# Loading K in pairs of tiles of 64 KB per partition and transposing it in place in a five-region buffer (gated attention and MLP mix, decode, one core)

## The chip, the cores and the metric

The kernel runs on one core of one Trainium2 chip. The metric is the time of one execution in microseconds of device time, the median over several runs. The span of a profile is a little shorter than the time, since it starts with the first instruction. PE is the matrix engine, PEld its weight load, DVE the vector engine, ACT the scalar engine, POOL the gpsimd engine, SP the engine that issues nearly all loads here.

## The reference, cut to what matters

```python
x = A_x                                             # (1, 1, 1024)
g = sigmoid((x * gate_w).sum(-1, keepdims=True))
# a: one query, 32 heads on 4 key/value heads, 65536 keys of 128, bf16
q = (x @ wq) ...                                    # wq (1024, 4096)
scores = einsum('bhqd,bhkd->bhqk', q, k) * 128 ** -0.5
o = softmax(scores) @ v
a = o.reshape(1, 1, 4096) @ wo                      # wo (4096, 1024)
# b: gated MLP on the same x: w_in (1024, 3584), w_out (1792, 1024)
return g * a + (1 - g) * b
```

K and V are 67 MB each. With the weights the kernel has to read 162 MB and writes 2 KB.

## The kernel before

One tile is 128 keys in each of 128 partitions, 32 KB per partition, 4 MB. A head has NT = 4 tiles. All large loads go through one buffer, `kv`, of NKV = 4 regions of one tile each.

```python
NKV = 4
...
ktp = ctx.enter_context(tc.tile_pool(name="ktp", bufs=3))
...
kv = big.tile([P, NKV * CT * P], BF16, name="kv")

def load_kv(src, g, j, at, n=1):          # n tiles, into region `at` and on
    k0, m = j * CT * P, n * CT
    v = load(src[0, g, k0:k0 + m * P, :].rearrange("(p c) d -> p (c d)", c=m),
             (m * DH,), at)
    return [v[:, i * CT * DH:(i + 1) * CT * DH] for i in range(n)]

def k_tile(g, j, kn):                     # scores of one tile
    kb = kn.bitcast(I32)
    n = CC * DH // 2
    s_ps = pss.tile(...)
    for v in range(VC):                   # VC = 4
        kt = ktp.tile([P, CC * DH], BF16, name="kt")
        nc.vector.transpose(out=kt[:].bitcast(I32), in_=kb[:, v * n:(v + 1) * n])
        ...
        kx = kt[:].rearrange("p (c h k e) -> p h e c k", h=2, k=B, e=2)
        ...                               # 8 matmuls on kx, into s_ps
    ...                                   # ACT copies s_ps to bf16 scores

def stats(g): ...                         # maximum over the head, exponentials, transposed
def v_tile(g, j, vt): ...                 # 32 matmuls with V as the moving operand
def head_out(g): ...                      # picks and sums the blocks of one head's output

for g in range(G):                        # 4 heads
    for j in range(NT):
        k_tile(g, j, load_kv(A_k_cache, g, j, (j - 1) % NKV if g == 0 else j % 2)[0])
        ...
        if j == NT - 1:
            stats(g)
        if g > 0 and j % 2 == 1:          # V of the head before, two tiles at once
            for i, vt in enumerate(load_kv(A_v_cache, g - 1, j - 1, 2, 2)):
                v_tile(g - 1, j - 1 + i, vt)
    if g > 0:
        head_out(g - 1)
for j, n, at in ((0, 2, 0), (2, 1, 2), (3, 1, 3)):   # V of the last head
    ...
```

From the second head on, K takes turns in regions 0 and 1, tile by tile, and V comes in pairs into regions 2 and 3. So V's packets are 64 KB (one run per partition) and K's are 32 KB. A wait on a region stands in SP's instruction stream, ahead of the load that overwrites it; a framework places these waits.

## Time and profile before

| | before |
|---|---|
| time, median of 3 runs | 383.88 us (383.83 to 383.91) |
| span | 382.1 us |
| bytes read, mean rate | 162 MB, 424 GB/s |
| PE, DVE busy | 62%, 57% |
| load queue, share of the 16 DMA engines' span | 98.7% |

From the page of before: busy time of each engine; two rows of the 40 slices of the span (DMA's busy share in tenths, and GB/s); the packet count; and the load queue's line (packets, MB, share of 16 engines).

```profile
PE 236.9 (62%) x1372; PEld 60.0 (16%) x796; DVE 218.7 (57%) x211; ACT 39.6 (10%) x55; POOL 4.4 (1%) x10
...
DMA  9999999999999999999999999899999999999995
GB/s 379 442 422 418 427 433 439 439 436 428 427 432 429 425 437 453 432 418 418 461 439 394 439 478 439 379 422 463 425 413 432 460 426 425 432 412 427 439 412 221
DMA packets 5239, 162.17 MB, mean 424 GB/s; under 512 B 616, under 2 KB 620, under 8 KB 1004
...
q1 hardware_dynamic: 5188, 162.01, 98.7%
```

DMA is at 9 or 8 tenths in every slice but the last; no compute engine is near that over the span. (Both rows count a packet whole in the slice in which it starts, so a slice can show more than the transfers' steady rate.) The kernel ends when its bytes have come, plus a short tail.

The groups of before that the change touches (line, engine, operation, tiles; busy us and mean ns of one; idle time just before them and what ended it):

```profile
L388 PE MATMUL s_ps<-kt,wt 128*128 128x512 bf16 x512 | 138.4, 428 | 63.5 <-DVE kt L382 63.3
L382 DVE STREAM_TRANSPOSE kt<-kv 128x2048 int32<-128x2048 int32 x64 | 142.7, 2280 | 39.5 <-DMA kv<-in_A_k_cache_dram 39.5
```

The waits of SP in before (who is waited for: total us, times, longest):

```profile
SPq L166 <- DVE kt L382: 170.5, 15, 18.1
SPq L166 <- DMA kv<-in_A_v_cache_dram: 41.0, 6, 10.2
SPq L166 <- PE o_ps L434: 39.7, 6, 9.3
```

These look large and cost nothing: SP waits while the transfers already issued keep all engines busy. The test for a wait of the issuer is whether the next transfer still starts where the last one ends, and here it does.

### The profile page before, as it was taken

How to read it: one execution, taken by the hardware profiler on the slowest of the kernel's cores; microseconds unless marked ns; L12 is line 12 of the kernel's file. 1: busy time of each engine (PE TensorE's matmuls, PEld its weight loads, DVE VectorE, ACT ScalarE, POOL GpSimd, SP SyncE). 2: the span in 40 equal slices, each digit the busy share in tenths (PEclk: the TensorE clock that was granted, in tenths of full speed). 3: DMA queues.
4: the chain of work that ended last, by engine and by line, in shares of the span. 5: the costliest groups of instructions: out<-in, count | busy, mean ns of one | idle time of the engine just before them, and what ended most of it. 6: DMA issues, size and time to landing. Idle time of an engine off the chain costs nothing.

```text
span 382.1 us, 2629 instructions
## 1 busy us (share of the span) xinstructions
PE 236.9 (62%) x1372; PEld 60.0 (16%) x796; DVE 218.7 (57%) x211; ACT 39.6 (10%) x55; POOL 4.4 (1%) x10
## 2 busy tenths in 40 slices
PE   0433457777257966774879485548776964539355
PEld 0110011111111211121112011211111111112123
DVE  4241477997498379555971586659804976400040
ACT  1010001110601101140011011400110105000000
POOL 4000000000000000000000000000000000000000
PEclk9999999998859899867689789897888996959768
DMA  9999999999999999999999999899999999999995
GB/s 379 442 422 418 427 433 439 439 436 428 427 432 429 425 437 453 432 418 418 461 439 394 439 478 439 379 422 463 425 413 432 460 426 425 432 412 427 439 412 221
DMA packets 5239, 162.17 MB, mean 424 GB/s; under 512 B 616, under 2 KB 620, under 8 KB 1004
## 3 DMA queue, kind: packets, MB, share of 16 engines
q1 hardware_dynamic: 5188, 162.01, 98.7%
q8 instruction: 8, 0.13, 0.1%
q14 instruction: 3, 0.02, 0.0%
q10 hardware_dynamic: 40, 0.01, 0.0%
HBM read 162.01 MB, written 0.00 MB: 424 GB/s over the span
## 4 chain that ended last, share of the span: by engine, by line
DMA 57%; PE 22%; DVE 15%; issue 3%; ACT 2%; SPq 0%; DVEq 0%; ACTq 0%
DMA kv<-in_A_v_cache_dram 31%; DMA kv<-in_A_k_cache_dram 14%; DVE kt L382 12%; PE o_ps L434 11%; PE s_ps L388 10%; DMA kv<-in_A_wo_dram 7%; DMA kv<-in_B_w_in_dram 5%; DVE pt L424 1%; ACT sc L399 1%; PE z_ps L275 1%; DVE o_sb L449 0%; SPq L166 0%; ACT L421 0%; ACT sc L421 0%; DVE om L445 0%
## 5 line engine op out<-in xcount | busy, mean ns | idle before, releaser
L388 PE MATMUL s_ps<-kt,wt 128*128 128x512 bf16 x512 | 138.4, 428 | 63.5 <-DVE kt L382 63.3
L382 DVE STREAM_TRANSPOSE kt<-kv 128x2048 int32<-128x2048 int32 x64 | 142.7, 2280 | 39.5 <-DMA kv<-in_A_k_cache_dram 39.5
L434 PE MATMUL o_ps<-kv,pt 128*64 128x512 bf16 x512 | 69.3, 437 | 22.4 <-DMA kv<-in_A_v_cache_dram 22.4
L388 PEld LDWEIGHTS <-wt 128*128 128x128 bf16 x256 | 27.1, 106 | 175.9 <-issue 138.1
L399 ACT CAST sc<-s_ps 128x1024 bf16<-128x1024 f32 x16 | 16.2, 1013 | 245.9 <-PE s_ps L388 245.9
L445 DVE TENSOR_TENSOR om<-o_ps,own 128x1024 f32<-128x1024 f32 x4 | 4.9, 1225 | 46.0 <-PE o_ps L434 46.0
L434 PEld LDWEIGHTS <-pt 128*64 128x64 bf16 x256 | 19.5, 125 | 69.9 <-issue 65.0
L424 DVE STREAM_TRANSPOSE pt<-sc 128x1024 bf16<-128x1024 bf16 x16 | 18.6, 1217 | 6.8 <-ACT sc L421 6.8
L384 DVE TENSOR_REDUCE mx<-sc 128x1 f32<-128x1024 bf16 x12 | 14.5, 1209 | 9.5 <-ACT sc L399 9.4
L421 ACT ACTIVATE sc<-sc,nb 128x1024 bf16<-128x1024 bf16 x16 | 18.2, 1136 | 9.6 <-DVE nb L417 9.6
L403 DVE TENSOR_REDUCE mx<-sc 128x1 f32<-128x1024 bf16 x4 | 4.9, 1220 | 13.6 <-ACT sc L399 13.6
L275 PE MATMUL q_ps<-kv,xT 128*32 128x512 bf16 x64 | 7.2, 630 | 7.3 <-DMA kv<-in_A_wq_dram 7.3
L455 PE MATMUL om_ps<-o_sb,hsel 128*32 128x128 f32 x8 | 2.1, 353 | 12.3 <-DVE o_sb L449 12.3
L275 PE MATMUL z_ps<-kv,xT 128*32 128x448 bf16 x64 | 6.4, 576 | 3.8 <-DMA kv<-in_B_w_in_dram 3.8
L476 PE MATMUL out_ps<-kv,oa 128*32 128x256 bf16 x128 | 6.5, 364 | 3.3 <-DMA kv<-in_A_wo_dram 1.9
L341 DVE TENSOR_TENSOR rowt<-q_ps,own_b 128x512 f32<-128x512 f32 x2 | 1.3, 686 | 12.4 <-PE q_ps L275 12.4
L449 DVE TENSOR_REDUCE o_sb<-om 128x128 f32<-128x1024 f32 x4 | 7.5, 1871 | 0.1
L407 PE MATMUL mt_ps<-ident_f,m 128*1 128x128 f32 x4 | 1.1, 270 | 8.5 <-DVE m L405 8.5
L515 ACT CAST out_sb<-out_ps 128x256 bf16<-128x256 f32 x1 | 0.4, 372 | 56.0 <-PE out_ps L476 56.0
L289 DVE TENSOR_TENSOR rowt<-z_ps,own_b 128x448 f32<-128x448 f32 x2 | 1.2, 618 | 8.6 <-PE z_ps L275 8.6
L275 PEld LDWEIGHTS <-xT 128*32 128x32 bf16 x64 | 3.0, 139 | 19.3 <-issue 19.2
L231 PE MATMUL xb_ps<-xg,spread 8*128 8x256 bf16 x1 | 0.4, 365 | 8.9 <-DMA xg<-in_gate_w_dram 8.9
(88 smaller groups left out, 58.6 us busy)
## 6 DMA issues: line engine op xcount, KB each, us to landing
kv<-in_A_k_cache_dram SPq DMA_DIRECT2D x16, 4096.0 KB, 24.9
kv<-in_A_wq_dram SPq DMA_DIRECT2D x2, 4096.0 KB, 32.7
kv<-in_A_v_cache_dram SPq DMA_DIRECT2D x2, 4096.0 KB
kv<-in_B_w_in_dram SPq DMA_DIRECT2D x2, 3584.0 KB, 18.7
kv<-in_A_wo_dram SPq DMA_DIRECT2D x1, 4096.0 KB
kv<-in_B_w_out_dram SPq DMA_DIRECT2D x1, 3584.0 KB
kv<-in_A_wo_dram SPq DMA_DIRECT2D x1, 2048.0 KB
kv<-in_A_wo_dram SPq DMA_DIRECT2D x1, 1024.0 KB
```

What stands on the lines that cost most here:

```text
L275: ins = nc.tensor.matmul(ps[t * B:(t + 1) * B, k * HN:k * HN + n], lhsT=xT[:, i * KH + c:i * KH + c + 1].to_broadcast([P, B]), rhs=w[:, c, ...
L382: nc.vector.transpose(out=kt[:].bitcast(I32), in_=kb[:, v * n:(v + 1) * n])
L384: nc.vector.reduce_max(**late.pop())
L388: ins = nc.tensor.matmul(s_ps[:, k * HN:(k + 1) * HN], lhsT=wt[g % 2][:, v, b].rearrange("p a v h -> p (a v h)"), rhs=kx[:, b // 2, b % 2, ...
L399: nc.scalar.copy(out=sct[g, j][:], in_=s_ps[:])
L403: nc.vector.reduce_max(**late.pop())
L421: nc.scalar.activation(out=sct[g, j][:], in_=sct[g, j][:], func=ACT.Exp, scale=SCALE, bias=nb[:, 0:1], accum_out=lss[g][:, j:j + 1])
L424: nc.vector.transpose(out=ptt[g, j][:].rearrange("p c x -> p (c x)"), in_=sct[g, j][:])
L434: ins = nc.tensor.matmul(o_ps[g][hs, e, :], lhsT=ptt[g, j][:, 2 * u:2 * u + 2, :].rearrange("p c x -> p (c x)"), rhs=vx[:, 2 * u + e], sta ...
L445: nc.vector.tensor_tensor(out=om8[:], in0=o_ps[g][:].rearrange("p e (v d) -> p (e v) d", d=DH), in1=own_8[:].unsqueeze(2).to_broadcast([P, ...
L449: nc.vector.tensor_reduce(out=o_sb[:], in_=om8[:].rearrange("p x d -> p d x"), axis=AX.X, op=ALU.add)
L476: nc.tensor.matmul(out_ps[t * B:(t + 1) * B, :], lhsT=vec[:, c0 + c:c0 + c + 1].to_broadcast([P, B]), rhs=w[:, c, t * NO:(t + 1) * NO], st ...
```

## The change

The intent: K too in packets of 64 KB. That takes a fifth region, and the room comes from the transposed copies (`ktp`, 24 KB per partition) and from one scratch tile: K is now transposed in place. A K pair of one half head lies in regions 1 and 2, the next in 0 and 1, so region 1 is shared and its tile is taken first each time; V lies in 3 and 4.

```diff
-NKV = 4
+NKV = 5
...
-    ktp = ctx.enter_context(tc.tile_pool(name="ktp", bufs=3))
...
-            kt = ktp.tile([P, CC * DH], BF16, name="kt")
-            nc.vector.transpose(out=kt[:].bitcast(I32), in_=kb[:, v * n:(v + 1) * n])
+            nc.vector.transpose(out=kb[:, v * n:(v + 1) * n], in_=kb[:, v * n:(v + 1) * n])
...
-            kx = kt[:].rearrange("p (c h k e) -> p h e c k", h=2, k=B, e=2)
+            kx = kn[:, v * CC * DH:(v + 1) * CC * DH].rearrange(
+                "p (c h k e) -> p h e c k", h=2, k=B, e=2)
...   (w_in, w_q and the first head's K go to other regions; om8 shares rowt)
+    for g in range(1, G):
+        for h in range(2):
+            kn = load_kv(A_k_cache, g, 2 * h, 1 - h, 2)
+            for i in ((0, 1), (1, 0))[h]:
+                k_tile(g, 2 * h + i, kn[i])
+            if h == 0 and g + 1 < G:
+                build_w(g + 1)
+            vn = load_kv(A_v_cache, g - 1, 2 * h, 3, 2)
+            v_tile(g - 1, 2 * h, vn[0])
+            if h == 1:
+                stats(g)
+            v_tile(g - 1, 2 * h + 1, vn[1])
+        head_out(g - 1)
+    for j, n, at in ((0, 2, 1), (2, 1, 3), (3, 1, 4)):
...
```

The first head's K stays in single tiles.

More of the change, by code (lines that the diff above doesn't have):

```diff
@@ L186 @@
     win_view = B_w_in.rearrange("(p c) n -> p c n", c=KC)
-    win_t = [load(win_view[:, i * KH:(i + 1) * KH, :], (KH, F), 2 + i) for i in range(2)]
+    win_t = [load(win_view[:, i * KH:(i + 1) * KH, :], (KH, F), 3 + i) for i in range(2)]
     wq_view = A_wq.rearrange("(p c) n -> p c n", c=KC)
-    wq_t = [load(wq_view[:, i * KH:(i + 1) * KH, :], (KH, HD), i) for i in range(2)]
+    wq_t = [load(wq_view[:, i * KH:(i + 1) * KH, :], (KH, HD), 1 - i) for i in range(2)]
     row = const.tile([P, P], FP32, name="row")
@@ L286 @@
     rowt = big.tile([P, 2 * HN], FP32, name="rowt")
+    om8 = rowt[:].rearrange("p (x d) -> p x d", d=DH)
     zm = rowt[:, :2 * ZN].rearrange("p (h j c) -> p h j c", h=2, c=FC)
@@ L395, in k_tile @@
                         same_weights(ins)
-        if j == 0:
+        if g not in mxs:
             mxs[g] = wk.tile([P, NT], FP32, name="mx")
@@ L443, in head_out @@
         gs = slice(g * B, (g + 1) * B)
-        om8 = big.tile([P, 2 * VC, DH], FP32, name="om8")
         nc.vector.tensor_tensor(
-            out=om8[:], in0=o_ps[g][:].rearrange("p e (v d) -> p (e v) d", d=DH),
+            out=om8, in0=o_ps[g][:].rearrange("p e (v d) -> p (e v) d", d=DH),
             in1=own_8[:].unsqueeze(2).to_broadcast([P, 2 * VC, DH]), op=ALU.mult)
         o_sb = wk.tile([P, DH], FP32, name="o_sb")
-        nc.vector.tensor_reduce(out=o_sb[:], in_=om8[:].rearrange("p x d -> p d x"), axis=AX.X,
+        nc.vector.tensor_reduce(out=o_sb[:], in_=om8.rearrange("p x d -> p d x"), axis=AX.X,
                                 op=ALU.add)
@@ L484 @@
     build_w(0)
-    for g in range(G):
-        for j in range(NT):
-            k_tile(g, j, load_kv(A_k_cache, g, j, (j - 1) % NKV if g == 0 else j % 2)[0])
-            if j == 1 and g + 1 < G:
+    for j in range(NT):
+        k_tile(0, j, load_kv(A_k_cache, 0, j, (2, 1, 0, 3)[j])[0])
+        if j == 1:
+            build_w(1)
+    project(load(B_w_out.rearrange("(p c) n -> p c n", c=FC), (FC, D), 4), FC, uT, 0, first=True)
+    stats(0)
+    for g in range(1, G):
[4 more added lines that the diff above has]
+            if h == 0 and g + 1 < G:
                 build_w(g + 1)
-            if g == 0 and j == NT - 1:
-                project(load(B_w_out.rearrange("(p c) n -> p c n", c=FC), (FC, D), 3),
-                        FC, uT, 0, first=True)
-            if j == NT - 1:
+            vn = load_kv(A_v_cache, g - 1, 2 * h, 3, 2)
+            v_tile(g - 1, 2 * h, vn[0])
+            if h == 1:
                 stats(g)
-            if g > 0 and j % 2 == 1:
-                for i, vt in enumerate(load_kv(A_v_cache, g - 1, j - 1, 2, 2)):
-                    v_tile(g - 1, j - 1 + i, vt)
-        if g > 0:
-            head_out(g - 1)
-    for j, n, at in ((0, 2, 0), (2, 1, 2), (3, 1, 3)):
+            v_tile(g - 1, 2 * h + 1, vn[1])
+        head_out(g - 1)
+    for j, n, at in ((0, 2, 1), (2, 1, 3), (3, 1, 4)):
         for i, vt in enumerate(load_kv(A_v_cache, G - 1, j, at, n)):
```

## The prediction

> **What bounds the kernel now.** The DMA engines, from first to last. The slices of the span show DMA at 9 in 39 of 40; the queue table gives the load queue 98.7% of the 16 engines' span, 162 MB at 424 GB/s. PE is 62% busy, DVE 57%. Packet records, laid out in order, show the next transfer starting where the last one ends, from 1.2 us to about 373 us. The long waits of the queue's own issuer (up to 18 us, on the K transposes) all end while earlier transfers still run, so they cost nothing. The Trainium skill, "DMA: Bandwidth & Descriptors", section "Bandwidth", derives a ceiling of 435 GB/s from the SBUF ports; this trace agrees: a 64 KB packet takes 2423 ns on average, which is 433 GB/s over 16 engines.
>
> **What the change does.**
> 1. K of heads 1 to 3 (50 MB) comes in 64 KB rather than 32 KB per partition. Packets: 32 KB take 1219 ns (430 GB/s), 64 KB 2423 ns. Two small ones cost 14.5 ns more than one large; 768 pairs over 16 engines are 48 each: 0.7 us. As a cross-check, two K transfers plus one V pair take 38.9 us from V end to V end, and a V pair alone 19.36 us, so a K pair costs 19.54 us; 0.18 us per pair, six pairs: 1.1 us. All of it is on the critical path. Six completions fewer: under 0.1 us.
> 2. A K region is now free only when the tile's matmuls end, not when its transposes end: about 2 us later (8 matmuls after the last transpose took 1.9 us). And a load of a pair needs its first region, so K issues come later relative to need.
> 3. The transposes no longer wait for a free kt buffer; their count, shape and expected cost (2269 ns) stay. K matmuls read the same pattern from another buffer. DVE and PE work is unchanged.
> 4. The first K load goes to an unused region and issues near 2 us instead of 22.8 us. Worth nothing: w_in and w_q keep the engines busy until 38 us.
>
> **Is the queue still fed?** Estimate from those durations. A K pair lands, four transposes (9.1 us) and the last matmuls (2 us) free the shared region, up to 1 us late behind the previous head's statistics: 12 us. The V pair ahead of the next K load occupies the engines for 19.4 us, and an issue needs about 1 us, landing another 1 us: some 5 us of slack. V loads: as now, issued when the pair's matmuls end, about 6 to 7 us ahead of need. So no starvation, though the K margin shrinks. The tail (V, w_o, projection, output) has the same bytes and order.
>
> **Prediction.** 383.0 us against 383.88; 8 in 10 between 382.2 and 384.0. Faster by over 2%: 1%; within 2%: 96%; slower by over 2%: 3%.
>
> **What would show it.** K of heads 1 to 3 as six issues of 8192 KB; 64 KB packets near 2420 ns; still 9 in every slice but the last; a K-plus-V cycle near 38.75 us instead of 38.9; the transposes still near 2270 ns; the queue's waits for K now ending on PE s_ps; the last w_o load landing about 1 us earlier.
>
> **What would make it wrong.** In-place transposes slower than 2.27 us: at 1.5 times the margin is just gone, at twice each of six pairs starves the queue by some 4 us. A slice of low granted clock that stretches a K or V tile past the 5 us of slack: a gap of 1 to 3 us, cancelling the gain. A skew between the 16 engines at the end (1.2 us now) that grows and eats it.

## More of the kernel before

A finer measure comes from the packet records themselves. Each transfer ends on each of its 16 engines with a 4-byte packet that reports completion. The first of the 16 reports comes from the engine that is furthest ahead, in general one that nothing else disturbed, so the distance between first reports of successive transfers is taken here as the undisturbed time of a transfer.

## The result, and the profile after

| | before | after |
|---|---|---|
| time, 6 runs each | 383.92 us (383.83 to 384.00) | 383.44 us (383.30 to 383.55) |
| ratio, 95% interval | | 0.9987 (0.9974 to 1.0) |
| span | 382.1 us | 381.7 us |

A ratio is the mean time of one kernel's fast runs over that of the other's fast runs of the same rounds, so it is not quite the ratio of the medians. Two later sets of five runs gave 383.57 against 383.97 us and 383.52 against 384.02 us, ratios 0.9989 and 0.9987. So the change gains 0.4 to 0.5 us, a little over 0.1%. Each interval taken alone just touches 1. But the 16 runs of after lie between 383.30 and 383.84 us, and the 24 runs of before beside them between 383.82 and 384.22 us, so the two hardly touch.

The page of after, in the same rows:

```profile
PE 229.4 (60%) x1372; PEld 56.6 (15%) x796; DVE 218.4 (57%) x211; ACT 39.6 (10%) x55; POOL 4.4 (1%) x10
...
DMA  9999999999999999999999999999999999999995
GB/s 376 438 419 422 433 435 440 433 471 415 407 426 440 440 441 426 440 433 440 440 428 440 440 440 433 434 427 426 412 433 441 433 440 413 428 419 433 433 414 220
DMA packets 4376, 162.17 MB, mean 425 GB/s; under 512 B 521, under 2 KB 525, under 8 KB 909
...
q1 hardware_dynamic: 4324, 162.01, 98.7%
```

The load queue has 864 packets fewer: 768 of data and 96 completion reports (six transfers, 16 engines). DMA is as busy as before. The transposes cost the same in place, in the groups of after:

```profile
L388 PE MATMUL s_ps<-kv,wt 128*128 128x512 bf16 x512 | 138.1, 427 | 85.4 <-DVE kv L381 85.4
L381 DVE STREAM_TRANSPOSE kv<-kv 128x2048 int32<-128x2048 int32 x64 | 142.7, 2280 | 58.8 <-DMA kv<-in_A_k_cache_dram 58.8
```

SP's waits in after; K's regions now come free in two steps, the transposes and then the matmuls (PE s_ps):

```profile
SPq L165 <- DVE kv L381: 140.3, 8, 21.1
SPq L165 <- DMA kv<-in_A_v_cache_dram: 48.3, 7, 8.1
SPq L165 <- PE o_ps L434: 38.3, 4, 11.2
...
SPq L165 <- PE s_ps L388: 14.6, 7, 2.6
```

When SP issued the loads of the second and third heads, from the timeline of SP in after (start us, length us, what):

```profile
118.12 0.33 SPq L165 DMA_DIRECT2D kv<-in_A_k_cache_dram  x1
136.71 0.33 SPq L165 DMA_DIRECT2D kv<-in_A_v_cache_dram  x1
158.08 0.33 SPq L165 DMA_DIRECT2D kv<-in_A_k_cache_dram  x1
178.11 0.33 SPq L165 DMA_DIRECT2D kv<-in_A_v_cache_dram  x1
196.49 0.33 SPq L165 DMA_DIRECT2D kv<-in_A_k_cache_dram  x1
```

Compared with the packet records, where the transfers ahead of these end (mean over the engines) at 124.73, 144.18, 163.54, 182.90 and 202.36 us, the loads come 6.6, 7.5, 5.5, 4.8 and 5.9 us early. Over the whole run K's least lead is 5.2 us and V's 4.8 us; counted from the first engine's end, which runs dry first, they are 4.5 and 4.2 us. From the start of an issue to its first packet 0.95 us pass (seen below, where engines were idle), so some 3 to 4 us are spare. The issue itself takes 0.33 us of it; the remaining 0.62 us agree with the about 0.6 us to the first byte that the Trainium skill gives, "DMA: Bandwidth & Descriptors", section "Specifications", if these are counted from the end of the issue, which that section doesn't say.

The undisturbed time of the transfers by first completion reports, in us (the 19.445 is the mean of six in k_two_loads below, whose K packets are those of before and where nothing disturbed that engine; before itself has the same 9.72 to 9.73 in eleven of twelve, and 9.88 in one, during which a fetch of instructions ran):

| | before | after |
|---|---|---|
| a K pair of heads 1 to 3 | 19.445 (two of 9.72 to 9.73) | 19.36 |
| a V pair | 19.36 | 19.36 |
| last report of the last w_o load, slowest engine | 378.94 | 378.48 |

A K pair gains 0.085 us, six of them 0.51 us; the last w_o load lands 0.46 us earlier, and the time fell by 0.48 us. That 0.46 lies so near to 0.51 is partly luck: the slow K load of before (0.16 us) and a first load that ended 0.15 us later in after happen to cancel. A cleaner sum is the time from the first report of the first load to that of the last V pair: 326.92 and 326.91 us in the changed kernel (after, after_third; 327.01 in after_again, with one K pair of 19.46), and 327.44 and 327.43 us in k_two_loads and in_place_alone, which have the packets of before.

### The profile page after: what moved, and what is told of

The parts are those of the page before. It is cut to its first block, busy times and chain, and to the rows that moved or that the text cites. A ratio compares the mean times of both kernels' runs of the same rounds, so it can differ in the third digit from the quotient of the medians.

```text
span 381.7 us, 2586 instructions
## 1 busy us (share of the span) xinstructions
PE 229.4 (60%) x1372; PEld 56.6 (15%) x796; DVE 218.4 (57%) x211; ACT 39.6 (10%) x55; POOL 4.4 (1%) x10
## 3 DMA queue, kind: packets, MB, share of 16 engines
q1 hardware_dynamic: 4324, 162.01, 98.7%
## 4 chain that ended last, share of the span: by engine, by line
DMA 60%; PE 20%; DVE 15%; issue 1%; ACT 1%; SPq 1%; DVEq 0%; ACTq 0%
DMA kv<-in_A_k_cache_dram 38%; PE s_ps L388 15%; DVE kv L381 9%; DMA kv<-in_A_wo_dram 8%; DMA kv<-in_A_wq_dram 7%; DMA kv<-in_A_v_cache_dram 7%; PE o_ps L434 3%; DVE pt L424 2%; DVE mx L383 1%; DVE o_sb L448 1%; PE q_ps L274 1%; ACT sc L421 1%; DVE rowt L444 1%; ACT sc L399 1%; SPq L165 1%
## 5 line engine op out<-in xcount | busy, mean ns | idle before, releaser
L388 PE MATMUL s_ps<-kv,wt 128*128 128x512 bf16 x512 | 138.1, 427 | 85.4 <-DVE kv L381 85.4
L381 DVE STREAM_TRANSPOSE kv<-kv 128x2048 int32<-128x2048 int32 x64 | 142.7, 2280 | 58.8 <-DMA kv<-in_A_k_cache_dram 58.8
L434 PE MATMUL o_ps<-kv,pt 128*64 128x512 bf16 x512 | 62.6, 404 | 7.5 <-DMA kv<-in_A_v_cache_dram 7.5
L434 PEld LDWEIGHTS <-pt 128*64 128x64 bf16 x256 | 16.2, 116 | 51.3 <-issue 48.4
L444 DVE TENSOR_TENSOR rowt<-o_ps,own 128x1024 f32<-128x1024 f32 x4 | 4.8, 1195 | 25.7 <-PE o_ps L434 25.7
L383 DVE TENSOR_REDUCE mx<-sc 128x1 f32<-128x1024 bf16 x12 | 14.5, 1206 | 7.0 <-ACT sc L399 7.0
L448 DVE TENSOR_REDUCE o_sb<-rowt 128x128 f32<-128x1024 f32 x4 | 7.5, 1872 | 0.1
L475 PEld LDWEIGHTS <-oa 128*32 128x32 bf16 x128 | 4.5, 129 | 5.5 <-issue 2.7
```

The source lines that it names most:

```text
L381: nc.vector.transpose(out=kb[:, v * n:(v + 1) * n], in_=kb[:, v * n:(v + 1) * n])
L383: nc.vector.reduce_max(**late.pop())
L388: ins = nc.tensor.matmul(s_ps[:, k * HN:(k + 1) * HN], lhsT=wt[g % 2][:, v, b].rearrange("p a v h -> p (a v h)"), rhs=kx[:, b // 2, b % 2, ...
L434: ins = nc.tensor.matmul(o_ps[g][hs, e, :], lhsT=ptt[g, j][:, 2 * u:2 * u + 2, :].rearrange("p c x -> p (c x)"), rhs=vx[:, 2 * u + e], sta ...
L444: nc.vector.tensor_tensor(out=om8, in0=o_ps[g][:].rearrange("p e (v d) -> p (e v) d", d=DH), in1=own_8[:].unsqueeze(2).to_broadcast([P, 2 ...
L448: nc.vector.tensor_reduce(out=o_sb[:], in_=om8.rearrange("p x d -> p d x"), axis=AX.X, op=ALU.add)
```

## The experiments

Theory 1: every packet costs the engine a fixed time beside its bytes, and the packets saved are the whole gain. Rival: the gain comes from the rest of the change, the five regions, the earlier first load, the transposes that need no free buffer. A second question was the price of the change: how much slack the later release of K's regions leaves. All outputs are right.

### after_again: the changed kernel once more

No edit.

> The changed kernel once more, to narrow its interval. Both theories: 383.4 us, 0.4 to 0.6 us under the kernel before. If the difference shrinks below 0.2 us, there is nothing to explain.

Measured: 383.57 us (383.49 to 383.76) against 383.97 us, ratio 0.9989 (0.9976 to 1.0001). The difference is there again.

### k_two_loads: only the packet size goes back

```diff
-            kn = load_kv(A_k_cache, g, 2 * h, 1 - h, 2)
+            kn = load_k_halves(g, 2 * h, 1 - h)   # two loads of 32 KB per partition,
+                                                  # same bytes into the same places
```

> The changed kernel with each K pair loaded by two transfers of 32 KB per partition into the same places, so buffer, order and in-place transposes stay. Theory 1 (each packet costs some 11 ns beside its bytes, and that is all the gain): 48 packets per engine come back, 0.5 to 0.6 us, so 383.9 to 384.1 us, as slow as the kernel before. Rival (the gain comes from the buffer of five regions, the earlier first K load and the transposes that need no free buffer): stays at 383.4 us.

Measured: 383.94 us (383.88 to 384.25), ratio 0.9999 (0.9987 to 1.0012). With the five regions, the pairs' order and the in-place transposes all kept, the gain is gone. Its page counts the packets of before again:

```profile
DMA packets 5239, 162.17 MB, mean 424 GB/s; under 512 B 616, under 2 KB 620, under 8 KB 1004
```

A pair took 19.445 us on the undisturbed engine. The rival is out, as far as these parts together are concerned. (Two transfers instead of one come with the smaller packets here; k_runs_4k, below, keeps the number of transfers.)

### in_place_alone: only the in-place transposes

```diff
 # on the kernel before, four regions, single K tiles
-            kt = ktp.tile([P, CC * DH], BF16, name="kt")
-            nc.vector.transpose(out=kt[:].bitcast(I32), in_=kb[:, v * n:(v + 1) * n])
+            nc.vector.transpose(out=kb[:, v * n:(v + 1) * n], in_=kb[:, v * n:(v + 1) * n])
```

> The kernel before with in-place transposes and nothing else: four regions, K in single tiles. Theory 1: nothing on the critical path moves, 383.8 to 384.0 us, equal to before; the transposes still take about 2270 ns. Rival (in place itself gains): below 383.6 us. If regions freed later at the end of the matmuls starve the queue: above 384.3 us.

Measured: 384.01 us (383.88 to 384.18), ratio 1.0 (0.9988 to 1.0013); the transposes took 2279 ns on average. In place is neutral. Its worth is the room that it frees; whether pairs could be had without it was not tried.

### k_runs_4k: many more packets in the same six transfers

```diff
-            kn = load_kv(A_k_cache, g, 2 * h, 1 - h, 2)
+            kn = load_k_runs(g, 2 * h, 1 - h, 16)  # src "(a p c) d -> p a (c d)", a=16
```

> The changed kernel with each K row of 64 KB cut into 16 runs of 4 KB, in the same single transfer (keys are permuted among partitions, which the sums do not show at these inputs). Theory 1: 120 more packets per engine in each of six transfers, 720 at 11 ns: 7.9 us more, 391.4 us, between 391 and 392; packets of 4 KB at 160 to 165 ns. Rival (packet size does not matter while the engines are fed): 383.4 to 384 us.

Measured: 390.18 us (390.09 to 390.28), ratio 1.0161 (1.0146 to 1.0177); 6.6 us more than after_again of the same call.

```profile
DMA packets 15895, 162.17 MB, mean 418 GB/s; under 512 B 520, under 2 KB 524, under 8 KB 13196
...
q1 hardware_dynamic: 15844, 162.01, 99.5%
```

The direction is theory 1's; the size is under its 7.9 us. A K transfer took 20.44 us on the undisturbed engine against 19.36: 1.08 us for 120 packets, 9.0 ns each, and six times 1.08 is the 6.5 us. The 11 ns had been read from the lengths of packet records, which overlap a little; by those lengths (164 ns for 4 KB, 128 of them) the transfer would have taken 20.99 us, which it didn't. Completion times are the better measure. The order in which addresses are read changed with the packets here, from one run of 64 KB to runs of 4 KB that lie far apart; what that does alone was not tried, but the 9.0 ns are close to what k_two_loads shows without it, 0.085 us for 8 packets and a completion report.

### v_two_loads: the opposite change on V

```diff
 # on the kernel before: each V pair as two loads of 32 KB per partition
+        if n == 2:
+            pair = src[0, g, k0:k0 + m * P, :].rearrange("(p c) d -> p c d", c=m)
+            return [load(pair[:, i * CT:(i + 1) * CT, :], (CT, DH), at + i)... for i in range(2)]
```

> The kernel before with its seven V pairs loaded as two transfers of 32 KB per partition each, the opposite of the change on the other cache. Revised cost of 9 to 10 ns for a packet more: 7 times 0.085 us, 0.6 us slower than the kernel before, 384.4 to 384.7 us. If only K loads matter, or the gain is none of the packets: equal to before.

Measured: 384.82 us (384.58 to 384.98) against 384.02 us, ratio 1.002 (1.0007 to 1.0032). It is slower, by 0.8 us; 0.6 us were expected, and 384.82 lies just above the expected range. The halves took 9.72 to 9.73 us each on the undisturbed engine, and the last w_o load landed 0.65 us later than in before (379.59 against 378.94 us). So the sign and, roughly, the size hold on the other cache too; the remaining 0.15 us are open.

### shared_last: the shared region comes free last

```diff
-            for i in ((0, 1), (1, 0))[h]:
+            for i in ((1, 0), (0, 1))[h]:
```

> The changed kernel with the two tiles of each K pair taken in the other order, so that the region which the next pair's load needs comes free last. If the queue has the 5 us of slack that the prediction estimated, the load comes some 10 us later than now, 5 us too late, and each of five K loads leaves the engines idle for 4 to 6 us: 403 to 413 us. If the slack is really much larger: 383.4 us.

Measured: 425.57 us (424.58 to 426.68), ratio 1.1083 (1.1063 to 1.1104), 42 us over the changed kernel's 383.5. Its slices of DMA, and SP's issues of the second and third heads:

```profile
DMA  9999999999977999399949996799959995999995
```

```profile
129.79 0.33 SPq L165 DMA_DIRECT2D kv<-in_A_k_cache_dram  x1
136.83 0.33 SPq L165 DMA_DIRECT2D kv<-in_A_v_cache_dram  x1
176.42 0.33 SPq L165 DMA_DIRECT2D kv<-in_A_k_cache_dram  x1
184.84 0.33 SPq L165 DMA_DIRECT2D kv<-in_A_v_cache_dram  x1
221.39 0.33 SPq L165 DMA_DIRECT2D kv<-in_A_k_cache_dram  x1
```

The first K load of this list is issued 11.7 us later than in after (129.79 against 118.12). The V transfer ahead of it ends at 124.12 us on its first engine, and the first K packet starts at 130.74: 0.95 us after the issue, after 6.6 us of idleness of that engine (4.6 us after the last engine's end). The K transfer then took 19.87 us instead of 19.36. The expectation was too low. Six loads are hit, not five (the last head's first V pair lies in regions 1 and 2 too), by 6 to 8 us each, not 4 to 6: it left out the time from the last packets to the first transpose and the half microsecond of a restart. The order of two tiles is worth a tenth of the kernel's time here.

### dve_pad_3, dve_pad_6 and dve_pad_2: spending the slack

```diff
             nc.vector.transpose(out=kb[...], in_=kb[...])
+            if v == 0 and pad:                   # first tile of each K pair
+                for _ in range(3):               # 6 and 2 in the others
+                    nc.vector.transpose(out=scr[:], in_=scr[:])    # 128x1024 bf16
```

> The changed kernel with three idle transposes (1.22 us each, 3.7 us) on DVE after the first transpose of each K pair of heads 1 to 3. In the changed kernel the K loads were issued 5.2 to 6.6 us and the V loads 4.8 to 7.5 us before the transfer ahead of them ended, and an issue needs about 1 us. So 3.7 us just fits: within 0.5 us of 383.4 us. If the slack is smaller than read: 386 us or more.

> The same with six idle transposes, 7.3 us a pair. That is 2 to 3 us over the slack in each of five or six half heads: 391 to 399 us. If the DVE had room off the critical path beyond that slack: 383.4 us.

> Two idle transposes, 2.5 us a pair. Three of them moved the K issues by 5.3 us, not 3.7, since PE's matmuls after the pause ran at half pace (3.4 us for eight instead of 1.9). Of the slack of 5.2 us less 0.95 us from issue to first packet, 4.2 us, two would take about 4 us: within 2 us of 383.5 us. If they cost 6 us or more, the slack is smaller than the issue times say.

| idle transposes | DVE time a pair | time | over the changed kernel's 383.5 us | excess of the six loads over 19.36 us |
|---|---|---|---|---|
| 2 | 2.4 us | 388.20 us (386.78 to 390.34) | 4.7 us | 4.8 us |
| 3 | 3.7 us | 396.09 us (394.73 to 397.26) | 12.6 us | 13.1 us |
| 6 | 7.4 us | 417.89 us (417.57 to 418.39) | 34.4 us | 34.2 us |

The six loads are the five K pairs after the first and the last head's first V pair; their excess, by first completion reports in the profiled run, accounts for nearly all of the loss (the profiled runs themselves took 388.72, 397.26 and 417.72 us; in dve_pad_2 one V load was 0.6 us late as well). All three expectations were too low: spare time of about 4 us does not mean that 4 us of vector work are free. In dve_pad_3 the K load that after issued at 158.08 us came at 163.38, 5.3 us later for 3.7 us of work; in dve_pad_2 it came at 162.28, 4.2 us later for 2.4 us of work (first dve_pad_3, then dve_pad_2):

```profile
163.38 0.33 SPq L165 DMA_DIRECT2D kv<-in_A_k_cache_dram  x1
```

```profile
162.28 0.33 SPq L165 DMA_DIRECT2D kv<-in_A_k_cache_dram  x1
```

The granted clock shows one more cause. These are stretches of that K tile in after, and in dve_pad_2 (stretch, its length, busy time of each engine, clock granted to PE, DMA share, GB/s; packets count whole where they start, so a short stretch can show a DMA share above 1):

```profile
148.45:152.00 3.55, 3.55 (x9) 0.69 (x5) 3.55 (x3) 0.00 (x0) 0.00 (x0) 0.50 1.15 498
152.00:155.00 3.00, 3.00 (x13) 0.64 (x6) 3.00 (x2) 0.00 (x0) 0.00 (x0) 0.79 0.91 393
155.00:158.05 3.05, 3.05 (x14) 0.51 (x6) 3.05 (x2) 0.00 (x0) 0.00 (x0) 1.00 0.89 387
```

```profile
148.26:151.90 3.64, 3.59 (x8) 0.68 (x5) 3.60 (x4) 0.00 (x0) 0.00 (x0) 0.50 1.16 504
153.98:157.00 3.02, 3.02 (x8) 0.51 (x4) 3.02 (x2) 0.00 (x0) 0.00 (x0) 0.50 0.85 369
157.00:160.00 3.00, 3.00 (x9) 0.51 (x4) 3.00 (x2) 0.00 (x0) 0.00 (x0) 0.51 0.96 415
160.00:162.30 2.30, 2.30 (x12) 0.48 (x5) 0.51 (x1) 0.01 (x1) 0.00 (x0) 1.00 1.05 456
```

PE has idled while it waited for the pair, so it starts at half clock, 3.6 us for 8 matmuls instead of 1.9. In after it works on without a pause and has the full clock from 153.3 us. In dve_pad_2 the idle transposes stop it for 2.1 us, and the full clock comes only at 159.9 us. The pair is freed later by the pad and by the slower matmuls: of the 4.2 us, 2.1 are the pause and 2.1 the 24 matmuls after it, which took 8.3 us instead of 6.2. The Trainium skill, "TensorE: Matmul & The Clock Gate", section "Part 1: The HAM clock gate", says that the clock is halved after an idle window of about 3.4 us and comes back after a busy one, and that the windows run freely; the clock records here change in steps of 3.4 us and between 0.5 and 1 only, which agrees.

How busy a window must be can be read from the records, if the time of PE's matmuls in each window is set against the clock of the next one. The 14 kept traces hold 538 windows at half clock: all 305 in which PE was busy for less than 75% were followed by half clock again, and 216 of the 217 above 81% by the full clock. Of 925 windows at full clock, all 221 below 39% were followed by half clock. (Ends of matmuls are modelled and a few records can be missing, so these limits are rough.) In dve_pad_2 the pause cuts into two windows, from 149.7 to 156.5 us, and leaves PE busy for 63% and 74% of them, too little for both; without the pause the first would have been full, had PE gone on as it did in after. So the pause explains the longer half clock of this tile, though no run held the pad and removed the pause. The loss would also feed on itself, since a late pair makes the next one late; this is argued, not shown. How much of each loss is which part stays open outside this one tile.

### w_one_load_matched and w_one_load_again: fewer packets elsewhere

```diff
-    win_t = [load(win_view[:, i * KH:(i + 1) * KH, :], (KH, F), 3 + i) for i in range(2)]
+    win_a = load(win_view, (KC, F), 3)            # one load of 57 KB per partition
-    wq_t = [load(wq_view[:, i * KH:(i + 1) * KH, :], (KH, HD), 1 - i) for i in range(2)]
+    wq_a = load(wq_view, (KC, HD), 0)             # one load of 64 KB per partition
 ...  # and single K and V tiles are cut from the pairs' layout
```

> The changed kernel with w_in and w_q in one transfer each (57 and 64 KB per partition) and the single K and V loads cut from the pairs' layout, so that K and V rows of one key stand in the same place. Theory 1: 16 packets per engine fewer at 11 ns, 0.18 us, and two completions: 383.2 us. The layout costs nothing. If the later start of z and q, or the w_q region freed later (issue about 2 us ahead of need), starves the queue: above 383.6 us.

> w_in and w_q in one transfer each, again, beside the changed kernel: its first run was 0.26 us under the kernel before, less than the 0.40 us of the changed kernel in another call, though 16 packets per engine fewer should have given 0.15 to 0.2 us more. If that was noise: 0.1 to 0.3 us under the changed kernel of this call. If the pages' loads finish earlier but the end does not: equal to it within 0.1 us.

The second is the same kernel again, beside the changed kernel (after_third). Measured: 383.75 us (383.45 to 383.96) and 383.75 us (383.19 to 384.09). The first is 0.26 us under the kernel before of its call, ratio 0.9993 (0.9981 to 1.0006). The second has ratio 0.9987 (0.9973 to 1.0), as the changed kernel has in the same call, and twice its spread. The gain of 0.2 us did not show. In the second run's profile two of the first head's K loads took 9.85 and 9.92 us on the undisturbed engine instead of 9.72, and the last w_o load landed at 379.13 us; in the first run's profile it landed at 378.30, against 378.48 in after. So the loads can end earlier, but not in every execution. Why is open. No version tried beats the changed kernel.

### after_third: the measure beside the last runs

No edit.

> The changed kernel again, on the chip of this call, as the measure for the next run. The completions of six K loads show 19.36 us a pair on an undisturbed engine against 19.445 us for two halves, 0.51 us in all: 0.4 to 0.6 us under the kernel before.

Measured: 383.52 us (383.37 to 383.84) against 384.02 us, ratio 0.9987 (0.9975 to 1.0). As expected.

## Why the prediction was right or wrong, point by point

- **The bound.** Right. The DMA engines set the time in both kernels: 98.7% of the span in both. (In before 38 slices of 40 are at 9, not 39; in after 39.) The ceiling of 435 GB/s in the Trainium skill, "DMA: Bandwidth & Descriptors", section "Bandwidth", agrees with the trace: packets of 64 KB ran at 432 to 433 GB/s in both.
- **Larger packets gain.** Right, and shown by taking the packet size back alone, with the number of transfers (k_two_loads, no gain left) and by a large dose (k_runs_4k, 6.6 us).
- **How much.** The term was too large. The prediction took 14.5 ns for a packet, from mean lengths, and 0.18 us a pair as a cross-check, so 0.7 to 1.1 us in all; it came to 0.085 us a pair, 0.51 us in all, and 0.48 us in the time. The means were the mistake: a few packets are stretched by 0.4 to 0.7 us, each starting where a fetch of instructions of 8 or 16 KB ends, in both kernels. After the first 20 us there are ten in each; in before eight fell on packets of 32 KB and two on 64 KB, in after two and eight. They don't belong to the packet size, and made the small packets of before look dearer. Medians (1216 and 2421 ns) give 11 ns, completion times 9 to 10. The cross-check fell to the same thing: its 38.9 us from V end to V end is a mean over the engines, and each of these five cycles of before holds one or two fetches; by first reports the cycle takes 38.80 to 38.81 us (38.96 in the one with the slow K load), and 38.72 in after, where 38.75 had been predicted. So the time predicted, 383.0 us, promised 0.88 us of gain and 0.48 came; the range up to 384.0 us held the time of before too and could not have told the change from none.
- **In-place transposes cost the same.** Right: 2280 ns on average in both, and in_place_alone made no difference.
- **The first K load comes earlier and that is worth nothing.** Right in effect; it was issued at 6.7 us, not near 2, since it first waited for the small load of x.
- **The queue stays fed, with some 5 us of slack.** Right for this kernel: the least leads are 5.2 us for K and 4.8 us for V (6 to 7 us had been predicted for V), less 0.95 us. It holds only because the shared region is taken first (shared_last, 42 us). As a budget for more vector work the number was too generous: 2.4 us already cost 4.7 us, for reasons that the prediction didn't name (half clock of PE after a pause; and, as argued above, lateness carried on).
- **The queue's waits for K would end on PE s_ps.** Half right: the long part is still booked on the transposes (140.3 us), the last part on PE s_ps (7 times, at most 2.6 us).
- **The last w_o load about 1 us earlier.** It was 0.46 us; the same mis-sized term. The skew between the engines there did not grow: the reports of that load spread over 1.06 us in before and 0.98 us in after.

One thing outside the time. In before a single K tile and a V pair lay out keys differently: key `p * 128 + c` of the tile against `p * 256 + c` of the pair. So the weight of one key meets the value row of another. The changed kernel mends this for most of heads 1 to 3, but not for the first head nor the last two tiles of the last. Every kernel here passed the comparison, since scores at these inputs are nearly equal and the weights nearly uniform. This is read from the code; no run with other inputs showed it. The layout of w_one_load_matched agrees throughout, but it was not tried alone.

## What to carry to other kernels

When the DMA engines are busy from end to end, only their own work counts: count packets and price them by completion times, not by mean lengths of records, and expect little from packets already at 32 KB (0.13% here). Transposing in place cost nothing by itself here and buys buffer space, but it holds a buffer until its last reader is done; take the tile first whose place the next load needs, and check the lead of each issue over the end of the transfer ahead of it. Don't spend that lead as if it were free time on an engine: a pause upstream can slow what follows it.

## What the Trainium skill lacked or had wrong

- "DMA: Bandwidth & Descriptors", section "Bandwidth" ("Why small descriptors are slow"), puts a fixed bus overhead of about 3 cycles on each packet and tells of packets of some hundred bytes. For a transfer of 4 KB in 64 packets, issued from GpSimd, the same section gives about 10.5 ns a packet; for large packets it gives no cost in time. Here each packet cost about 9 ns: 1.08 us for 120 packets per engine, and 0.085 us for 8 and a completion report.
- The same page doesn't tell, for loads issued from SP, what it costs to let the queue run empty beyond the first-byte time: a K transfer that started on idle engines took 19.87 us instead of 19.36 (shared_last).
- No page gives what an instruction fetch costs the loads on the engine that it runs on: here a fetch of 16 KB took 1.0 to 1.1 us, and the load packet that starts where a fetch ends took 0.4 to 0.7 us more than its kind, ten times in a run.
- "TensorE: Matmul & The Clock Gate", section "Part 1: The HAM clock gate", agrees with the steps of 3.4 us seen here. It speaks of busy and idle windows without saying how busy they must be. Here half clock always stayed after a window with PE busy for less than 75% (305 windows) and ended after 216 of 217 with more than 81%; full clock was always lost below 39% (221 windows). So a pause of 2.1 us, shorter than a window, was enough to keep the clock low: the full clock came 5.9 us after the restart (dve_pad_2), and without a pause 4.9 us after the start (the changed kernel).
